# Attention by pairs of heads: both heads' float32 scores and value products alternate between the halves of the array

## The chip, the cores and the metric

One core of one Trainium2 chip. The metric is the device time of one execution in microseconds (us), the median of three runs; lower is better.

## What is computed

Windowed causal attention with a linear bias (4 batches, 8 heads, 576 positions, 64 dimensions per head, window 128), then two dense layers over the 2304 tokens.

```python
scores = q @ k.T / sqrt(64)
scores = where((rel >= 0) & (rel < 128), scores - slope[h] * abs(rel), -1e9)
attn = softmax(scores)                      # per head
x = concat_heads(attn @ v)                  # (2304, 512)
g = x @ w_gate                              # (2304, 1536)
x = (g * sigmoid(g) * (x @ w_val)) @ w_out  # (2304, 512)
h = x @ w_in                                # (2304, 2048)
out = (h * tanh(softplus(h))) @ w_out2      # (2304, 512)
```

## The kernel before, in words

The tokens are cut into five chunks of 512, 384, 512, 512 and 384 (`A_CHUNKS`, line 25), numbered 0 to 4. Per chunk `attention` (L138) makes x, kept as a high and a low float32r half, and the gated layer follows: `gv_groups` (L604) issues 24 hidden groups of 12 matmuls in PSUM tiles `g_ps` (L573), and `out_group` (L637) 12 groups of 12 into `acc`. The attention of chunk 0 runs first and alone ("the start"). After that the attention of chunk c+1 is cut into pieces that are woven between the groups of chunk c's gated layer: the loop at L985 gives out pieces in proportion to their estimated costs. The order on TensorE is written out by hand (`manual_schedule`, L912); a scheduler orders the other engines. Conversions of 64-bit weights to float32 halves (`convert`, L409), on ScalarE and VectorE, are handed out in small steps in between (`pump`). After the gated layer comes a second layer (`layer2`, L756), whose matmuls write tiles `bk`.

`chunk_plan` (L38) cuts a chunk into query blocks of 128 or 64 rows, with 128 to 256 key columns each, packed in PSUM banks of 512 columns. The score columns of a head, by bank, are: chunk 0: 256 and 256, 256 and 128; chunk 1: 256 and 192, 192 and 128; chunk 2: 256 and 256, 256 and 128; chunk 3: 256 and 256, 192, 192 and 128; chunk 4: 256 and 256, 256. Blocks of 192 have 64 query rows. The columns of a head's value products, from key blocks of 128 rows, are: chunk 0: 256, 256, 256, 128; chunk 1: 256, 192, 64; chunk 2: 256, 256, 128, 128, 128; chunk 3: 256, 192, 192, 128; chunk 4: 256, 256, 128, 128. Chunks 1 and 3 have two more blocks of 64 rows and 64 columns each.

The work of a head h has these parts:
- `load` (L147), on the SP queue. In the first `S_FULL` pairs of a chunk (all four in chunk 0, two in chunk 1, none after) a pair of heads is loaded once into 128 partitions, one head in each half of 64. Otherwise each head's q and k are loaded twice, into both halves.
- `split` (L183). For pairs loaded once ScalarE scales q (L188). For the others ScalarE rounds q and k (L196, L124), and VectorE makes what rounding left: the lower half of `Q` (L198) and `KL` (L127).
- `score` (L204), bank by bank into `s_ps`, one of four rotating PSUM banks (`rot`, L119): one float32 product of 64 rows for pairs loaded once; for the others two float32r products over 128 rows, with `K1` and with `KL`. In the trace a float32 product is two MATMULs, a float32r one is one. VectorE adds the bias and takes the minimum (L226), ScalarE makes exponentials with their sums (L230) into `Pt` (10 buffers).
- `norm` (L236): VectorE makes the reciprocals (L238, L241); POOL in chunk 0 (L249) and ScalarE after it (L247) multiply.
- `transp` (L251): TensorE transposes into `t_ps`, ScalarE copies to `PT` (L271).
- `outp` (L274), per pair: the value products, first of one head into partitions 0 to 63 of `o_ps`, then of the other into 64 to 127; ScalarE and VectorE make the halves of x.

`attention_pieces` (L298) orders these as S, T and O pieces by head. In each step "SSOTT" takes the scores of head st, the transposes of the head one before it (two in chunk 0), and the value products one step later again.

Of the kernel before, what the change touches and what calls it, by code (L numbers as in the profile page):

```python
# [9 lines left out]
F32 = mybir.dt.float32  # L10
# [15 lines left out]
S_FULL = [4, 2, 0, 0, 0]  # L26
# [6 lines left out]
    order="SSOTT", delay0=2, early=[4], pbufs=10, pump_g=2, pump_p=2, lag=4, lastlag=6, evprio=500,  # L33
# [4 lines left out]
def chunk_plan(t0, n):  # L38
# [53 lines left out]
    o_order = sorted(kb, key=lambda x: x.par)  # L92
# [4 lines left out]
def body(ctx: ExitStack, tc: tile.TileContext, qT, kT, vP, w1, w1o, w2, cst, yT):  # L97
# [40 lines left out]
    def attention(ap, p, ci, s_native, upfront):  # L138
# [5 lines left out]
        def s_full(h):  # L144
            return h // 2 < s_native

        def load(h):  # L147
            pr, e = divmod(h, 2)
            if s_full(h) and e:
                return  # L150
# [4 lines left out]
            elif s_full(h):  # L155
                q = ap.tile([128, p.n], F32, tag=("qraw", "Q")[pr % 2], name="q32")
                k = ap.tile([128, p.nk], F32, tag=("K1", "KL")[pr % 2], name="k32")
            else:
                q = ap.tile([128, p.n], F32, tag="qraw", name="qraw")
                k = ap.tile([128, p.nk], F32, tag="kraw", name="kraw")  # L160
            for s in p.segs:
                cq, ck = slice(s.c0, s.c0 + s.n), slice(s.koff, s.koff + s.kn0 + s.n)
                sq, sk = slice(s.s0, s.s0 + s.n), slice(s.s0 - s.kn0, s.s0 + s.n)
                if s_full(h):
                    nc.sync.dma_start(out=q[:, cq], in_=qT[s.b, h:h + 2, :, sq].rearrange("h d s -> (h d) s"))
                    nc.sync.dma_start(out=k[:, ck], in_=kT[s.b, h:h + 2, :, sk].rearrange("h d s -> (h d) s"))
                    continue
                for e in range(2):
                    nc.sync.dma_start(out=q[64 * e:64 * e + 64, cq], in_=qT[s.b, h, :, sq])
                    nc.sync.dma_start(out=k[64 * e:64 * e + 64, ck], in_=kT[s.b, h, :, sk])  # L170
            raw[h] = (q, k)
# [11 lines left out]
        def split(h):  # L183
            c = -float(2.0 ** (h - 2))
            if s_full(h):
                if h % 2 == 0:
                    q, k = raw.pop(h)
                    nc.scalar.activation(out=q, in_=q, func=AF.Copy, scale=qsc[:, h // 2:h // 2 + 1])  # L188
                    for e in range(2):
# [888 lines left out]
```

## Time and profile before

| | |
|---|---|
| median of three runs | 1001.56 us (1001.00, 1001.56, 1004.53) |
| span of the profiled execution | 1002.2 us; no other time of it is listed |
| busy: PE, DVE, ACT, POOL | 966.8, 706.7, 555.0, 137.4 us |
| start (chunk 0's attention alone) | 0 to 58.85 us |
| windows with attention woven in | 58.85 to 556.8 us |
| gated layer of chunk 4, then second layer | from 556.8 us |

PE is TensorE's matmuls and PEld its weight loads, DVE VectorE, ACT ScalarE, POOL GpSimd, SP the queue that issues transfers; L117 is a helper through which nearly all matmuls go, so tile names tell them apart. Matmuls overlap: the ends of their records are modelled, so the time that a group takes is read from its first start to the start of what comes next. The granted clock is a share of 2.4 GHz.

### The profile page before, as it was taken

How to read it: one execution, taken by the hardware profiler on the slowest of the kernel's cores; microseconds unless marked ns; L12 is line 12 of the kernel's file. 1: busy time of each engine (PE TensorE's matmuls, PEld its weight loads, DVE VectorE, ACT ScalarE, POOL GpSimd, SP SyncE). 2: the span in 40 equal slices, each digit the busy share in tenths (PEclk: the TensorE clock that was granted, in tenths of full speed). 3: DMA queues.
4: the chain of work that ended last, by engine and by line, in shares of the span. 5: the costliest groups of instructions: out<-in, count | busy, mean ns of one | idle time of the engine just before them, and what ended most of it. 6: DMA issues, size and time to landing. Idle time of an engine off the chain costs nothing. (4 is left out here: it accounts for less than half of the span.)

```text
span 1002.2 us, 14578 instructions
## 1 busy us (share of the span) xinstructions
PE 966.8 (96%) x5168; PEld 854.4 (85%) x5168; DVE 706.7 (71%) x1263; ACT 555.0 (55%) x1135; POOL 137.4 (14%) x204
## 2 busy tenths in 40 slices
PE   6899999999999999999999999899999999999998
PEld 4557777898997877788787999789999999999998
DVE  4989898686586644647843576787795888867773
ACT  6857566666677555544643345555463555545342
POOL 2610000000000000000001233454002330022000
PEclk8989999999999999999999999999999999999999
DMA  8854433566454632326610898432787137850275
GB/s 303 283 208 146 136 120 114 183 214 199 129 166 152 215 110 69 101 65 227 233 43 22 298 374 293 169 116 84 243 260 254 64 109 269 291 172 22 82 248 195
DMA packets 76920, 174.82 MB, mean 174 GB/s; under 512 B 9136, under 2 KB 52528, under 8 KB 67120
## 3 DMA queue, kind: packets, MB, share of 16 engines
q1 hardware_dynamic: 76848, 173.90, 51.9%
q8 instruction: 40, 0.66, 0.3%
q14 instruction: 32, 0.26, 0.1%
HBM read 138.22 MB, written 35.65 MB: 173 GB/s over the span
## 5 line engine op out<-in xcount | busy, mean ns | idle before, releaser
L117 PE MATMUL g_ps<-xt,w 128*128 128x512 f32 (+1 forms) x1440 | 316.4, 372 | 1.1 <-ACT PT L271 1.1
L117 PEld LDWEIGHTS g_ps<-xt,w 128*128 128x128 f32 x1440 | 258.4, 188 | 38.0 <-ACT PT L271 2.2
L117 PE MATMUL bk<-xs,win 128*128 128x384 f32 x1008 | 179.1, 336 | 7.5 <-DVE G L679 5.4
L117 PEld LDWEIGHTS bk<-xs,win 128*128 128x128 f32 x1008 | 174.4, 188 | 11.8 <-DVE G L679 9.0
L117 PE MATMUL bk<-op,wout 128*128 128x384 f32 x1008 | 175.5, 334 | 0.5 <-DMA wout<-w2o 0.5
L117 PEld LDWEIGHTS bk<-op,wout 128*128 128x128 f32 x1008 | 174.8, 188 | 0.8 <-issue 0.8
L117 PE MATMUL acc<-hh,ring 128*128 128x512 f32 (+1 forms) x480 | 149.4, 374 | 1.6 <-DVE ring L127 1.6
L124 ACT ACTIVATE op<-G 128x768 fp32r<-128x768 f32 x84 | 70.8, 846 | 65.6 <-PE bk L117 63.1
L117 PEld LDWEIGHTS acc<-hh,ring 128*128 128x128 f32 x480 | 88.9, 188 | 15.4 <-DVE ring L127 2.3
L127 DVE TENSOR_TENSOR op<-G,op 128x768 fp32r<-128x768 f32 x84 | 80.5, 965 | 26.9 <-ACT op L124 26.3
L117 PE MATMUL acc<-hl,ring 128*128 128x512 f32 (+1 forms) x240 | 88.4, 368 | 0.0
L230 ACT ACTIVATE Pt<-Pt,sm 128x256 f32<-128x256 f32 (+2 forms) x160 | 74.3, 466 | 14.8 <-DVE sm L226 14.5
L613 ACT ACTIVATE t<-g_ps 128x512 f32<-128x512 f32 (+1 forms) x60 | 32.9, 549 | 78.8 <-PE g_ps L117 78.6
L614 DVE SCALAR_TENSOR_TENSOR t<-t,g_ps 128x512 f32<-128x512 f32 (+1 forms) x60 | 37.7, 629 | 53.0 <-ACT t L613 53.0
L226 DVE CUSTOM_DVE_ANT_0 Pt<-s_ps,cst_sb 128x256 f32<-128x256 f32 (+2 forms) x160 | 54.2, 376 | 27.7 <-PE s_ps L117 19.4
L775 POOL TENSOR_TENSOR t<-w 128x256 f32<-128x256 f32 x48 | 42.5, 905 | 224.1 <-DVE win L127 211.3
L622 DVE SCALAR_TENSOR_TENSOR t<-t,g_ps 128x512 f32<-128x512 f32 (+1 forms) x60 | 37.9, 632 | 37.0 <-PE g_ps L117 36.0
L1023 ACT ACTIVATE G<-G 128x384 f32<-128x384 f32 x72 | 36.8, 520 | 44.4 <-DVE G L679 44.4
L679 DVE TENSOR_TENSOR G<-u,bk 128x384 f32<-128x384 f32 x72 | 39.0, 552 | 31.3 <-PE bk L117 29.2
L124 ACT ACTIVATE hh<-t 128x512 fp32r<-128x512 f32 (+1 forms) x60 | 34.9, 582 | 43.8 <-DVE t L622 43.8
L259 PE MATMUL t_ps<-cst_sb,Pt 128*128 128x128 f32 (+2 forms) x288 | 47.0, 279 | 7.7 <-POOL Pt L249 4.2
L247 ACT ACTIVATE Pt<-Pt,sm 128x256 f32<-128x256 f32 (+2 forms) x128 | 50.1, 465 | 7.1 <-DVE sm L241 7.0
(75 smaller groups left out, 1250.8 us busy)
## 6 DMA issues: line engine op xcount, KB each, us to landing
wout<-w2o SPq DMA_DIRECT2D x42, 1024.0 KB, 6.4
wraw<-w SPq DMA_DIRECT2D x16, 1024.0 KB, 5.7
w2o<-chl SPq DMA_DIRECT2D x16, 896.0 KB, 8.7
wst<-w SPq DMA_DIRECT2D x12, 1024.0 KB, 7.4
cw<-w1od SPq DMA_DIRECT2D x24, 512.0 KB, 3.9
w<-w2d SPq DMA_DIRECT2D x24, 512.0 KB, 3.3
w2d<-cw SPq DMA_DIRECT2D x16, 512.0 KB, 4.6
wraw<-w1o SPq DMA_DIRECT2D x6, 1024.0 KB, 6.1
```

Of the source, the lines that this page charges most:

```text
L117: nc.tensor.matmul(out=out, lhsT=lhsT, rhs=rhs, start=start, stop=stop, skip_group_check=True)
L124: return nc.scalar.activation(out=out, in_=in_, func=AF.Copy)
L127: return nc.vector.tensor_tensor(out=out, in0=in_, in1=hi.bitcast(F32), op=ALU.subtract)
L226: nc.vector.tensor_tensor_reduce(out=Pt[:q.qn, :w], in0=s_ps[:q.qn, q.so:q.so + w], in1=nb[:q.qn, 128 - q.kn:128 + q.qn], op0=ALU.add, op1 ...
L230: nc.scalar.activation(out=Pt[:q.qn, :w], in_=Pt[:q.qn, :w], func=AF.Exp, scale=-1.0, bias=sm[:q.qn, i:i + 1], accum_out=sm[:q.qn, 8 + i:9 ...
L247: nc.scalar.activation(out=pt, in_=pt, func=AF.Copy, scale=r)
L259: nc.tensor.transpose(t_ps[:x.n, o:o + q.qn], Pt[:q.qn, c0:c0 + x.n], ident[:q.qn, :q.qn])
L614: nc.vector.scalar_tensor_tensor(out=t[:, :n], in0=t[:, :n], scalar=1.0, in1=st["g"][:, :n], op0=ALU.add, op1=ALU.mult)
L622: nc.vector.scalar_tensor_tensor(out=t[:, :n], in0=t[:, :n], scalar=0.5, in1=vps[:, :n], op0=ALU.mult, op1=ALU.mult)
L679: nc.vector.tensor_tensor(out=out, in0=a, in1=b, op=op)
L775: nc.gpsimd.tensor_tensor(out=x[:, o], in0=a, in1=b, op=ALU.subtract)
L1023: nc.scalar.activation(out=out, in_=in_, func=AF.Mish)
```

## The change

Every pair of heads in every chunk is loaded once and scored in float32, without rounded halves. A score piece takes a bank for both heads of a pair, two PSUM banks, and alternates between the heads block by block. One reciprocal step serves a pair. The value products alternate between the heads too, blocks of 128 rows first. Pieces are ordered by pair: "OSTTSTT" takes the value products of two pairs before, a score bank, transposes of the pair before, and so on. Costs of pieces are worked out anew. `Pt` has 16 buffers, `sm` 3, q and k two each. Cut to its core:

```diff
-    order="SSOTT", delay0=2, early=[4], pbufs=10, pump_g=2, pump_p=2, lag=4, lastlag=6, evprio=500,
+    order="OSTTSTT", early=[2], pbufs=16, pump_g=2, pump_p=2, lag=4, lastlag=6, evprio=500,
...
-    o_order = sorted(kb, key=lambda x: x.par)
+    o_order = sorted(kb, key=lambda x: (x.n != 128, x.par))
...
+                nc.sync.dma_start(out=q[:, cq], in_=qT[s.b, hs_, :, sq].rearrange("h d s -> (h d) s"))
+                nc.sync.dma_start(out=k[:, ck], in_=kT[s.b, hs_, :, sk].rearrange("h d s -> (h d) s"))
+            raw[pr] = (q, k)
...
-            nc.scalar.activation(out=Q, in_=q, func=AF.Copy, scale=c)
-            hi_act(K1, k)
-            nc.vector.scalar_tensor_tensor(
-                out=Q[64:128], in0=q[64:128], scalar=c, in1=Q[64:128].bitcast(F32), op0=ALU.mult, op1=ALU.subtract
-            )
-            lo_dve(KL, k, K1)
-            qk[h] = (Q, K1, KL)
+        def split(pr):
+            q, k = raw.pop(pr)
+            nc.scalar.activation(out=q, in_=q, func=AF.Copy, scale=qsc[:, pr:pr + 1])
+            qk[pr] = (q, k)
+
+        def score(pr, g):
             blocks = p.sb[g][0]
+            s_ps = [rot("s_ps") for _ in range(2)]
...
             for q in blocks:
                 w = q.kn + q.qn
-                    mm(o, Q[:, q.c:q.c + q.qn], K1[:, q.ko:q.ko + w], True, False)
-                    mm(o, Q[:, q.c:q.c + q.qn], KL[:, q.ko:q.ko + w], False, True)
+                for e in range(2):
+                    r = slice(64 * e, 64 * e + 64)
+                    mm(s_ps[e][:q.qn, q.so:q.so + w], Q[r, q.c:q.c + q.qn], K[r, q.ko:q.ko + w], True, True)
...
-            for e in range(2):
-                st = True
-                for x in p.o_order:
-                    c0 = x.uses[0][0].c
+            for i, x in enumerate(p.o_order):
+                c0 = x.uses[0][0].c
+                for e in range(2):
                     mm(
                         o_ps[64 * e:64 * e + 64, c0:c0 + x.w], v[:x.n, x.vi, 64 * e:64 * e + 64],
-                        pt_[2 * pr + e, x.bank][:x.n, x.bo:x.bo + x.w], st, False,
+                        pt_[2 * pr + e, x.bank][:x.n, x.bo:x.bo + x.w], i == 0, False,
                     )
...
+            return (a.ci, sum(max(2 * (q.kn + q.qn), 256) for q in a.p.sb[g][0]) / 1200, f)
...
-            return (a.ci, a.nk * 0.86, f)
+            return (a.ci, a.nk * 0.46, f)
...
-            bufs = {"P": CFG["pbufs"], "sm": 8, "PT0": 2, "PT1": 2}
+            bufs = {"P": CFG["pbufs"], "sm": 3, "PT0": 2, "PT1": 2, "q": 2, "k": 2}
```

## Rows read from the trace of the kernel before

**Rows 1.** The page: its head, and busy time of PE with its share.

```profile
span 1002.2 us, 14578 instructions
...
PE 966.8 (96%) x5168; PEld 854.4 (85%) x5168; DVE 706.7 (71%) x1263; ACT 555.0 (55%) x1135; POOL 137.4 (14%) x204
```

**Rows 2.** Busy time by stage; behind the engines: granted clock, transfers' share, GB/s.

```profile
0.00:58.85 58.85, 43.48 (x184) 29.32 (x184) 42.79 (x118) 41.62 (x102) 27.22 (x52) 0.85 0.88 308
58.85:194.30 135.45, 132.82 (x637) 98.94 (x637) 119.98 (x242) 90.61 (x207) 1.49 (x10) 1.00 0.43 141
194.30:299.70 105.40, 102.73 (x637) 97.68 (x637) 73.74 (x173) 71.20 (x175) 0.83 (x8) 1.00 0.54 169
299.70:436.90 137.20, 137.20 (x674) 106.28 (x673) 75.22 (x173) 75.82 (x196) 0.92 (x6) 1.00 0.38 121
436.90:556.80 119.90, 118.35 (x581) 96.03 (x581) 69.06 (x131) 57.83 (x123) 3.90 (x5) 1.00 0.37 122
```

**Rows 3.** Matmuls of s_ps in two stretches of the start (length, PE busy, count).

```profile
6.58:7.86 1.28, 1.28 (x4) 1.00 0.90 277
7.86:9.14 1.28, 1.28 (x8) 1.00 1.10 287
```

**Rows 4.** The same for o_ps, later in the start.

```profile
34.70:35.38 0.68, 0.68 (x4) 1.00 1.01 364
35.38:36.06 0.68, 0.68 (x8) 1.00 0.99 398
```

**Rows 5.** Matmuls of o_ps by window (length, PE busy, count).

```profile
58.85:194.30 135.45, 13.73 (x81) 1.00 0.43 141
194.30:299.70 105.40, 11.49 (x80) 1.00 0.54 169
299.70:436.90 137.20, 17.07 (x96) 1.00 0.38 121
436.90:556.80 119.90, 8.89 (x64) 1.00 0.37 122
```

**Rows 6.** Timeline of PE (start, length): first and last of five float32 score matmuls.

```profile
30.43 0.38 PE L117 MATMUL s_ps<-qkv 64*128 64x256 f32 x1
...
31.30 0.38 PE L117 MATMUL s_ps<-qkv 64*128 64x256 f32 x1
```

**Rows 7.** Timeline of PE: a rounded head's 512 score columns, to the next group.

```profile
452.74 0.28 PE L117 MATMUL s_ps<-K,Q 128*128 128x256 f32 x1
...
453.22 0.40 PE L117 MATMUL acc<-hh,ring 128*128 128x512 f32 x1
```

**Rows 8.** Timeline of PE: gated groups and float32 scores; an undisturbed run of 24.

```profile
58.86 3.03 PE L117 MATMUL g_ps<-xt,w 128*128 128x512 f32 x12
61.81 1.16 PE L117 MATMUL s_ps<-k,q 64*128 64x256 f32 x4
62.90 0.50 PE L117 MATMUL g_ps<-xt,w 128*128 128x512 f32 x1
...
137.03 5.66 PE L117 MATMUL g_ps<-xt,w 128*128 128x512 f32 x24
142.53 0.27 PE L259 MATMUL t_ps<-cst_sb,Pt 128*128 128x128 f32 x1
```

**Rows 9.** Groups of DVE, 58.85 to 194.30 us (busy, mean ns, idle before).

```profile
L441 DVE SCALAR_TENSOR_TENSOR cw<-cw,cp 128x1024 f32<-128x1024 f32 x15 | 18.2, 1213 | 0.1
...
L127 DVE TENSOR_TENSOR KL<-kraw,K 128x512 fp32r<-128x512 f32 (+1 forms) x7 | 5.2, 741 | 0.1
L198 DVE SCALAR_TENSOR_TENSOR Q<-qraw,Q 64x384 fp32r<-64x384 f32 (+1 forms) x7 | 4.3, 613 | 0.2
```

**Rows 10.** Waits of PE over the span (us in total, times, longest).

```profile
PE s_ps L117 <- DVE Q L198: 2.1, 2, 1.3
```

**Rows 11.** The start: groups of POOL to 58.85 us; timeline of PE, last value products.

```profile
L249 POOL TENSOR_SCALAR Pt<-Pt,sm 128x256 f32<-128x256 f32 (+1 forms) x32 | 25.5, 813 | 25.5 <-ACT qkv L188 10.8 <-DVE sm L241 8.0 <-PE o_ps L117 4.7
...
54.10 4.83 PE L117 MATMUL o_ps<-PT,qkv 128*64 128x256 f32 x16
```

More of the change, by code (lines that the diff above doesn't have):

```diff
@@ L136, in body, with attention, load @@
     x_t = {}
-    def attention(ap, p, ci, s_native, upfront):
+    def attention(ap, p, ci, upfront):
         raw, qk, pt_, P_, sums = {}, {}, {}, {}, {}
         nb_ = len(p.qb)
[L144 to L150, printed above, removed]
+        def load(pr):
             if upfront:
@@ new lines, in norm @@
+        def norm(pr):
+            sm = sums.pop(pr)
+            nc.vector.tensor_scalar(out=sm[:, 16:32], in0=sm[:, 16:32], scalar1=1.0e-9, scalar2=None, op0=ALU.add)
+            nc.vector.reciprocal(out=sm[:, 32:48], in_=sm[:, 16:32])
+            for e in range(2):
+                for q in p.qb:
+                    w = q.kn + q.qn
+                    i = 32 + 8 * e + q.idx
+                    Pt = P_[2 * pr + e, q.idx]
+                    pt, r = Pt[:q.qn, :w], sm[:q.qn, i:i + 1]
+                    if ci:
+                        nc.scalar.activation(out=pt, in_=pt, func=AF.Copy, scale=r)
+                    else:
+                        nc.gpsimd.tensor_scalar(out=pt, in0=pt, scalar1=r, scalar2=1.0, op0=ALU.mult, op1=ALU.mult)
@@ L298, in attention_pieces, with load @@
     def attention_pieces(atts):
-        heads = [(a, h) for a in atts for h in range(H)]
         pairs = [(a, r) for a in atts for r in range(HP)]
-        n = len(heads)
+        n = len(pairs)
         out = []
         def run(k, f):
-            a, h = heads[k]
-            return getattr(a, f)(h)
-        def load(k):
-            if not heads[k][0].upfront:
-                run(k, "load")
-        def load_v(r):
-            if not pairs[r][0].upfront:
-                pairs[r][0].load_v(pairs[r][1])
+            a, r = pairs[k]
+            return getattr(a, f)(r)
+        def load(k, *fs):
+            if not pairs[k][0].upfront:
+                for f in fs:
+                    run(k, f)
         def first():
             if atts[0].upfront:
-                for h in range(0, H, 2):
-                    run(h, "load")
-                    for f in early.pop(h, []):
-                        f()
-            load(0)
-            load_v(0)
+                for r in range(HP):
+                    run(r, "load")
+                    for f in early.pop(r, []):
+                        f()
+            load(0, "load", "load_v")
             run(0, "split")
-            load(1)
-            load_v(1)
+            load(1, "load", "load_v")
         def s_piece(k, g):
-            a, h = heads[k]
+            a, r = pairs[k]
             def f():
@@ L340, in f @@
                         if k + 2 < n:
-                            load(k + 2)
-            return (a.ci, 1.7 if a.s_full(h) else 0.87, f)
+                            load(k + 2, "load")
+            return (a.ci, sum(max(2 * (q.kn + q.qn), 256) for q in a.p.sb[g][0]) / 1200, f)
         def o_piece(k):
-            a, h = heads[k]
+            a, r = pairs[k]
             def f():
```

125 lines of the change are left out of this document (38 added, 87 removed).

## The prediction

> **What bounds the kernel now.** I read the page's busy shares first: TensorE is busy 96% of a span of 1002.2 us [rows 1]. An average hides stages, so next came the table by stage [rows 2]. It has five stages up to 556.8 us: the start, in which the attention of token chunk 0 runs alone, and four windows, in each of which the gated layer of one chunk runs while the attention of the next is woven in. What follows is not touched. The reader is to see three things there. In the start TensorE is busy only 43.48 of 58.85 us, and no engine is full: VectorE 42.79, ScalarE 41.62, at a mean granted clock of 0.85. From 194.3 us on TensorE alone is full (102.73 of 105.40, 137.20 of 137.20, 118.35 of 119.90) and VectorE is at 55 to 70%. In the window from 58.85 to 194.30 us both are close: TensorE 132.82 and VectorE 119.98 of 135.45. So TensorE time taken out of the last three windows is time off the end; in the first it is so only as far as VectorE follows.
>
> **Do halves of the array run side by side?** On this the change stands, and the kernel before already shows it where two neighbouring score groups of heads 0 and 1 meet. Two stretches of equal length hold 4 and then 8 float32 score matmuls [rows 3]: the second head, on the other 64 rows, starts beside the first. The value products show the same for the column halves, where the second head of a pair begins before the first ends: 4, then 8 in 0.68 us [rows 4]. Neither shows a slower pace. It happens only at the seams because all of one head is issued before the other; alternating makes it last through the group.
>
> **Value products (the large gain).** By stage their matmuls are busy 13.73, 11.49, 17.07 and 8.89 us, 51.2 in all [rows 5]. The pace of a float32 matmul of 256 columns comes from two starts four apart, 30.43 and 31.30 [rows 6]: 0.87 / 4 = 0.217 us; each product issues two, so 0.43 us per 256 columns. With both heads abreast a pair costs one head's columns. Chunk 1: 512 columns from 128-row blocks, 0.87 us, and two 64-column blocks of 64 rows, four matmuls at 0.11 (an estimate: twice the column share of 0.217). Chunk 2: 896 columns, 1.52. Chunk 3: 768, 1.30, and again two small blocks. Chunk 4: 768, 1.30. For going in and out I add 0.25 us, and 0.15 for the change from 128 to 64 rows, estimates from the changes of shape below. That is 1.7, 1.8, 2.1 and 1.55 us a pair, times four pairs: 28.6. Gain: 51.2 - 28.6, rounded to **-22 us**. Bounds: -12, if only every other block finds its neighbour, to -25 without the 0.25 and 0.15.
>
> **Scores (a loss on balance).** Chunks 2 to 4 and half of chunk 1 now pay two float32r matmuls per block; a head's 512 columns take 452.74 to 453.22 us, 0.48 [rows 7], or 0.96 for two heads. In float32 the same 512 columns take 4 x 0.217 = 0.87 for both heads together, nearly the same, but changing the array's shape costs. One head's float32 group of 448 columns lasts from 61.81 to 62.90, 1.09 us, of which 0.76 is columns; the 12 matmuls ahead of it last 58.86 to 61.81, 2.95, against half of 5.50 (137.03 to 142.53) where nothing changes shape [rows 8]. So 0.33 + 0.20, with 0.1 for the second head's tail: 0.63 us per group. A pair has two groups. After, per pair: chunk 1: 768 columns, 1.30 + 1.26 = 2.56; chunk 2: 896, 2.78; chunk 3: 1024, 2.99; chunk 4: 768, 2.56; times four, 43.6 us. Before: rounded pairs 1.44, 1.68, 1.92, 1.44; in chunk 1 two pairs were float32 head by head, 2 x (1.30 + 2 x 0.53) = 4.7 each. Sum 9.4 + 2.9 + 4 x 5.04 = 32.5. That is +11; groups whose blocks are all 128 wide spare the second change of shape inside the 0.33, so I take **+8 us**, bounds +3 (changes of shape half hidden) and +11.
>
> **Halves no longer made.** In the first window alone VectorE loses 5.2 + 4.3 = 9.5 us [rows 9]; ScalarE's rounding and the doubled loads of q and k go too. Off the path this is worth nothing by itself, since TensorE covers it. But TensorE waited 2.1 us for those halves [rows 10], and this goes: **-2**. What is late next there is the scale of q, one ScalarE instruction per pair, issued a whole pair ahead.
>
> **VectorE in the first window.** TensorE's work there falls by some 9 us: 7 from value products, 1 from scores, 1 from the wait. VectorE's falls by 9.5 of 119.98, so it stays as full as it was; its conversions, 1.213 us an instruction [rows 9], hold up what TensorE asks for. I give back **+2**, bounds 0 and +8.
>
> **The start.** Its last value product group takes 54.10 to 58.86, 4.76 us, for 16 matmuls, straight before the first gated matmul [rows 8, 11]; abreast, at the same clock, seven units of 0.43 and 0.4 around them, 3.4: -1.4. The other three groups and the scores of four pairs lose about half too, but beside ScalarE and VectorE. Against this, normalising on POOL (32 instructions, 25.5 us, 0.813 each [rows 11]) now follows both heads' scores, so the first transposes can wait for up to four more, 3.3 us, once. Bounds: -10 (TensorE's idle 15.4 us largely closed up) to +6 (late by a head at two stages). I take **-4**, nearer to the last group, whose saving is plain. The remaining edits I cost at nothing. Loads go from two a head and segment, or four, to two a pair; on SP such a load now waits for the scores of two pairs before, to reuse their q and k, and weight loads queue behind it. What hides this is a lead of a whole pair and transfers that fill only 0.37 to 0.54 of the windows [rows 2]; without it a window's conversion would start late, by one load. The sixteen score buffers for ten hold two pairs, as ten held two heads and a half.
>
> The start's clock is a reason for doubt. The row shows a mean of 0.85 of 2.4 GHz before the gated layer and 1.00 in every later window [rows 2]: it stood at 1.2 GHz for part of a stretch with much idle TensorE. The Trainium skill (TensorE: Matmul & The Clock Gate, section Part 1: The HAM clock gate) says that the throttled state is the default and that activity releases it; by that, a start with less matmul work would sit lower still, and the sum would be some 6 us higher. The trace agrees only in that the clock is lower where TensorE idles.
>
> **Sum.** -22 + 8 - 2 + 2 - 4 = -18 on the span of 1002.2, 984.2. The median of the runs shown, 1001.56, lies 0.6 below that span, so **983.5 us**. Everything after 556.8 us moves up unchanged: its weight combinations begin only when the attention's memory is free.
>
> **Rivals.**
> Gains close up further (970 us): start -10, scores +3, nothing given back: -31 in all. For it: every stage of the start waits. Against: VectorE's 120 us in the first window. Chance 0.17.
> Pairs are too coarse (993 us): the start ends 6 later instead of 4 earlier. For it: POOL's chain; against: TensorE and ScalarE have less to do. 0.13.
> The start runs mostly at 1.2 GHz (989.5 us): transposes and value products lie between POOL and the first gated matmul. Price: of the 43.48 us that TensorE is busy some 31 stay; from a clock of 0.85 to 0.5 they take 22 longer, and I count a quarter of that as on the path, as TensorE idles a quarter of the start (15.4 of 58.85) [rows 2]: +6. For it: the clock of 0.85. Against: the scores of both heads, now back to back. 0.07.
> Slower, by PSUM banks (up to 1023 us): a score group of a pair now takes two of the four rotating banks, so the next hidden group or transposes meet a bank sooner that VectorE hasn't read. Place: behind the 32 score groups of the windows. Price: one long conversion, 1.213 us [rows 9], each, 39 us. It decides from 18 / 32 = 0.56 us per group on. For it: the first window, where VectorE is full. Against: the other windows with VectorE at 55 to 70% [rows 2]. 0.05.
> The halves take turns after all (1024 us), and the change doesn't do what it says: value products keep 51.2 us, scores of both heads are paid in full, about +19 more. Against it stand 8 in the place of 4 [rows 3, 4]. 0.03.
>
> **Numbers.** The forecast's case has 0.55, its own range 976 to 991. From the fast rival to the coarse pairs with their bounds the range is 970 to 996; outside lie the last two and some of either end, under 0.2. A measurement of this kernel can tell about 0.5%, 5 us: faster than 996.5 are the forecast, the fast one, the clock and most of the coarse: 0.87; within it 0.07; slower 0.06.
>
> **What would show it.** Value products busy near 29 us over the four windows; a score group of 512 columns for two heads in 1.1 to 1.4 us; no Q or KL rows on VectorE; the gated layer starting near 55 us; the first window near 128 us long, then about 102, 132 and 121. It is wrong if the starts of the two heads' matmuls follow each other instead of pairing, if TensorE's waits for VectorE's reading of score banks grow to over 10 us, or if the start is longer than 58.85.

## The result, and the profile after

The changed kernel takes 1009.2 us in the median of five runs (1007.69 to 1014.23); the kernel before, run again beside it, 1001.56. The ratio is 1.0073, with a 95% interval of 1.0047 to 1.0099: a little slower, where 983.5 us had been forecast. The profiled run is itself the one of 1009.2 us, with a span of 1007.4.

The page of the changed kernel: its head, the busy times, and the granted clock over 40 slices.

```profile
span 1007.4 us, 14079 instructions
...
PE 949.3 (94%) x5168; PEld 828.8 (82%) x5168; DVE 665.8 (66%) x1167; ACT 532.5 (53%) x1093; POOL 133.2 (13%) x184
...
PEclk7889999999999999999999999999999999999999
```

Every engine has less to do than before [rows 1]: TensorE 17.5 us less, VectorE 40.9, ScalarE 22.5. The time grew all the same: over the span TensorE stands idle for 58.1 us, against 35.4 before, so it lies in waits. The table by stage, with the columns PE, PEld, DVE, ACT, POOL, clock, transfers' share and GB/s, says where:

```profile
0.00:62.20 62.20, 35.85 (x185) 22.77 (x185) 42.44 (x110) 42.85 (x103) 25.25 (x43) 0.81 0.79 282
62.20:196.10 133.90, 128.22 (x638) 95.00 (x638) 107.27 (x213) 83.59 (x196) 0.56 (x5) 0.97 0.38 125
196.10:302.80 106.70, 102.58 (x638) 92.94 (x637) 61.47 (x149) 64.70 (x163) 0.45 (x4) 0.98 0.46 150
302.80:435.50 132.70, 131.11 (x674) 99.01 (x673) 67.34 (x153) 69.43 (x185) 0.45 (x4) 1.00 0.34 115
435.50:560.00 124.50, 119.44 (x582) 92.89 (x580) 62.67 (x115) 54.05 (x114) 3.93 (x5) 0.99 0.32 107
```

Against [rows 2] the start is 3.3 us longer (62.20 for 58.85). The four windows together last 497.8 us, against 497.95: nothing was gained. What follows 560 us takes 447.4 us, 2.0 more than before. In the windows TensorE idles 16.4 us (497.8 less the sum of its busy times, 481.4), against 6.9 before; and its clock, which stood at 1.00 in every window, is now 0.97, 0.98, 1.00 and 0.99. Each share missing, times its window, is 4.0 + 2.1 + 0 + 1.2 = 7.4 us of full speed lost, before rounding. I use these two sums, **idle** and **lost clock**, for every kernel below; the shares have two decimals, so a lost clock is good to some 2 us.

The TensorE work itself did become cheaper. The sum over the four windows for the value products:

```profile
sum 497.80, PE 31.27 PEld 19.93 DVE 10.60 ACT 9.24; mean PE 7.82 PEld 4.98 DVE 2.65 ACT 2.31
```

The same for the scores:

```profile
sum 497.80, PE 34.94 PEld 19.76 DVE 41.71; mean PE 8.74 PEld 4.94 DVE 10.43
```

Value products: 31.3 us for the 51.2 of [rows 5]. Scores: 34.9, where the same view of the kernel before sums to 42.5. Counted from the start of a score group to the start of what follows it, with idle time taken off, which leaves overlap out, it is 32.9 against 34.5. What TensorE waits for in the windows (us in total, times, longest):

```profile
PE o_ps L116 <- ACT PT L239: 8.2, 6, 2.9
PE t_ps L227 <- DVE t L569: 4.0, 1, 4.0
PE g_ps L116 <- DVE sm L193: 1.4, 2, 0.7
PE t_ps L227 <- ACT Pt L215: 1.2, 1, 1.2
PE s_ps L116 <- DVE t L577: 1.0, 1, 1.0
```

And the largest in the start:

```profile
PE t_ps L227 <- POOL Pt L217: 17.2, 9, 6.0
```

The largest in the windows is new: the value products wait for `PT`, the copies of the transposes. Three of the others, 4.0, 1.4 and 1.0 us, are waits for a PSUM bank that VectorE has not read yet. A wait for `PT` on TensorE's timeline (start, length; in brackets the wait and what ended it):

```profile
320.95 0.91 PE L227 MATMUL t_ps<-cst_sb,Pt 128*128 128x128 f32 x4
...
324.75 0.97 PE L116 MATMUL o_ps<-PT,v 128*64 128x256 f32 x6
326.81 1.46 PE L116 MATMUL o_ps<-PT,v 128*64 128x192 f32 x18 [1.09 <-ACT PT L239]
```

ScalarE's timeline beside it:

```profile
322.78 3.66 ACT L215 ACTIVATE Pt<-Pt,sm 128x256 f32<-128x256 f32 x10
326.34 0.53 ACT L239 ACTIVATE PT<-t_ps 128x320 f32<-128x320 f32 x2
```

The transposes are done by 321.86, but ScalarE copies them only at 326.34. Ahead of the copies in its queue stand the ten normalisations of the next pair, 3.66 us in one burst. Some of these waits TensorE pays for a second time. The table of TensorE around a wait of 2.90 us for the same copies (length, busy, clock, transfers):

```profile
286.00:289.90 3.90, 3.90 (x26) 1.00 0.26 92
289.90:294.10 4.20, 1.30 (x13) 0.97 0.00 0
294.10:297.50 3.40, 3.40 (x17) 0.54 0.14 36
297.50:301.00 3.50, 3.50 (x22) 1.00 0.27 76
```

After 2.90 idle of 4.20 us the granted clock is 0.54 for the next 3.40 us, near the lower of its two levels, 1.2 GHz, with TensorE busy all the time; then it is full again.

### The profile page after: what moved, and what is told of

Its sections match the earlier page's. It is cut to its first block, busy times and chain, and to the rows that moved or that the text cites. A ratio compares the mean times of both kernels' runs of the same rounds, so it can differ in the third digit from the quotient of the medians.

```text
span 1007.4 us, 14079 instructions
## 1 busy us (share of the span) xinstructions
PE 949.3 (94%) x5168; PEld 828.8 (82%) x5168; DVE 665.8 (66%) x1167; ACT 532.5 (53%) x1093; POOL 133.2 (13%) x184
## 4 chain that ended last, share of the span: by engine, by line
PE 72%; DVE 8%; DMA 8%; ACT 6%; issue 3%; POOL 2%; SPq 1%; DVEq 0%; ACTq 0%; POOLq 0%
PE bk L116 30%; PE g_ps L116 24%; PE acc L116 11%; DMA wraw<-w 4%; PE o_ps L116 2%; PE s_ps L116 2%; PE t_ps L227 2%; ACT Pt L215 2%; ACT Pt L198 1%; POOL Pt L217 1%; POOL t L730 1%; DVE cw L390 1%; DMA x2d<-ev 1%; DMA w<-w2d 1%; DVE G L634 1%
## 5 line engine op out<-in xcount | busy, mean ns | idle before, releaser
L116 PE MATMUL g_ps<-xt,w 128*128 128x512 f32 (+1 forms) x1440 | 320.3, 376 | 1.4 <-DVE sm L193 1.4
L116 PE MATMUL acc<-hh,ring 128*128 128x512 f32 (+1 forms) x480 | 153.2, 382 | 1.6 <-DVE ring L126 1.6
L116 PEld LDWEIGHTS acc<-hh,ring 128*128 128x128 f32 x480 | 90.5, 191 | 16.4 <-DVE ring L126 2.3
L198 ACT ACTIVATE Pt<-Pt,sm 128x256 f32<-128x256 f32 (+2 forms) x160 | 74.2, 465 | 30.8 <-DVE sm L193 30.7
L227 PE MATMUL t_ps<-cst_sb,Pt 128*128 128x128 f32 (+2 forms) x288 | 51.2, 290 | 22.7 <-POOL Pt L217 17.2
L126 DVE TENSOR_TENSOR hl<-t,hh 128x512 fp32r<-128x512 f32 (+1 forms) x60 | 40.1, 669 | 47.3 <-ACT hh L123 47.3
L568 ACT ACTIVATE t<-g_ps 128x512 f32<-128x512 f32 (+1 forms) x60 | 32.9, 548 | 71.3 <-PE g_ps L116 71.2
L227 PEld LDWEIGHTS t_ps<-cst_sb,Pt 128*128 128x128 f32 (+2 forms) x288 | 34.8, 144 | 42.5 <-POOL Pt L217 22.4
L577 DVE SCALAR_TENSOR_TENSOR t<-t,g_ps 128x512 f32<-128x512 f32 (+1 forms) x60 | 37.7, 628 | 36.5 <-PE g_ps L116 35.4
```

What stands on the lines that cost most here:

```text
L116: nc.tensor.matmul(out=out, lhsT=lhsT, rhs=rhs, start=start, stop=stop, skip_group_check=True)
L126: return nc.vector.tensor_tensor(out=out, in0=in_, in1=hi.bitcast(F32), op=ALU.subtract)
L198: nc.scalar.activation(out=Pt[:q.qn, :w], in_=Pt[:q.qn, :w], func=AF.Exp, scale=-1.0, bias=sm[:q.qn, i:i + 1], accum_out=sm[:q.qn, 16 + i: ...
L227: nc.tensor.transpose(t_ps[:x.n, o:o + q.qn], Pt[:q.qn, c0:c0 + x.n], ident[:q.qn, :q.qn])
L568: tanhs.append(nc.scalar.activation(out=t[:, :n], in_=st["g"][:, :n], func=AF.Tanh, scale=0.5))
L577: nc.vector.scalar_tensor_tensor(out=t[:, :n], in0=t[:, :n], scalar=0.5, in1=vps[:, :n], op0=ALU.mult, op1=ALU.mult)
```

## The experiments

Times are medians; every ratio is against the kernel before, run on the same chip. Windows means the sum of the four windows.

### Which part pays, and which costs

**e3: the kernel before, with the value products alternating and nothing else.**

```diff
-    o_order = sorted(kb, key=lambda x: x.par)
+    o_order = sorted(kb, key=lambda x: (x.n != 128, x.par))
...
-            for e in range(2):
-                st = True
-                for x in p.o_order:
+            for i, x in enumerate(p.o_order):
+                for e in range(2):
...
-            return (a.ci, a.nk * 0.86, f)
+            return (a.ci, a.nk * 0.46, f)
```

> The kernel before with one part of the change: value products alternate between the heads, blocks of 128 rows first, piece cost 0.46; scores, order by head and buffers as before. Theory (the gain of 22 us of TensorE time is real and is kept where value products stand a head's step behind their transposes): value products busy near 30 us in the windows, under 9 us idle on TensorE there, time 983 (979 to 988). Rival (VectorE and transfers set the pace of the windows): time 996 to 1001.

981.84 us, ratio 0.9821 [0.9773, 0.9869]. The sum of its windows by engine:

```profile
sum 474.80, PE 469.39 PEld 384.93 DVE 335.87 ACT 292.33 POOL 7.12; mean PE 117.35 PEld 96.23 DVE 83.97 ACT 73.08 POOL 1.78
```

The same for its value products alone:

```profile
sum 474.80, PE 26.64 PEld 17.38 DVE 10.62 ACT 9.09; mean PE 6.66 PEld 4.34 DVE 2.65 ACT 2.27
```

The windows are 23.2 us shorter than before, for 24.5 us of value products: here the gain reaches the end. Idle 5.4, lost clock 2.0.

**e4: the changed kernel, with the value products head by head again** (the same lines, reversed).

> The changed kernel with the value products one head after the other again, as before the change. Theory (their halved time was mostly given back as waits for PT copies, which a longer first head would cover): waits of value products fall under 2 us and no stretches at 1.2 GHz follow them; TensorE works 20 us longer; time 1016 (1012 to 1021). Rival (the gain is kept in full and the 27 us that are missing are lost elsewhere): 1027 to 1032.

1035.89 us, ratio 1.0333 [1.0308, 1.0358]; both figures missed, and the rival's by less. The value products are worth 26.7 us in the pairs' order too. So it is the rest, the pairs' scores and their order, that costs some 30.

**e9: e3 with float32 scores in all chunks, head after head.**

```diff
-S_FULL = [4, 2, 0, 0, 0]
+S_FULL = [4, 4, 4, 4, 4]
```

> The best version so far (value products alternating, scores and order by head as before, 981.8 us) with float32 scores in all five chunks, head after head: the rounded halves of q and k are gone here too, but the steps stay those of one head. The run with the pairs' scores head after head (1019.5 us) has the same score matmuls in the order by pairs. Theory (the order by pairs is what costs, not the float32 scores): the four windows stay near 475 us; blocks of 64 rows double the pace of their groups, which added 10.5 us to the windows of that run, half of it here since chunk 1 had half of its heads so already; 2 to 3 us of waits for the halves go: 985 us, between 980 and 992. Rival (the float32 scores, or what VectorE and ScalarE do in the freed time, cost it): 1000 to 1015 us, with the stretches at 1.2 GHz in the windows and waits for VectorE as in the changed kernel.

1019.11 us, ratio 1.0169 [1.0139, 1.02]: above both. Of the rival's two reasons it is the first, the scores themselves; the waits for VectorE that it named don't come. Idle stays at 5.3 us, but the scores take TensorE 66.75 us, against 42.85 in e3. The sum over its windows for the scores:

```profile
sum 511.00, PE 66.75 PEld 37.58 DVE 43.77; mean PE 16.69 PEld 9.39 DVE 10.94
```

The windows grow by 36.2 us against e3. From start to start the scores take 61.6 us of them, for 33.7 in e3, and the groups between them the other 8.

**e5: the changed kernel, with the score matmuls of one head after those of the other** inside a step.

```diff
-            for q in blocks:
-                w = q.kn + q.qn
-                for e in range(2):
+            for e in range(2):
+                for q in blocks:
+                    w = q.kn + q.qn
```

> The changed kernel with the score matmuls of a piece in turn: first all blocks of one head, then all of the other, in the same two banks. Theory (TensorE looks some four matmuls ahead, so in a short group the second head starts while the first head's last matmuls still wait, with or without alternation): a group of 512 columns for two heads stays under 1.4 us for 1.06, time 1008 to 1014. Rival (only alternation makes the halves run side by side): such a group takes 1.9 us, 32 groups some 25 us, time 1030 to 1036.

1019.45 us, ratio 1.0172 [1.0141, 1.0203], between the two. Groups of blocks of 128 rows don't mind (1.07 us for 1.06); those with blocks of 64 rows double (2.41 for 1.22). So the alternation is needed for float32 scores to cost TensorE no more than rounded ones, and it delivers that. The loss must come from somewhere else.

### Repairs of the changed kernel

**e1: value products behind the first two transposes, three buffers for `PT`** (the start as it was).

```diff
+    order="STTOSTT", order0="OSTTSTT", early=[2], pbufs=15, pump_g=2, pump_p=2, lag=4, lastlag=6, evprio=500,
...
+            for c in CFG["order0"] if st < 5 else CFG["order"]:
...
+            bufs = {"P": CFG["pbufs"], "sm": 3, "PT0": 3, "PT1": 3, "q": 2, "k": 2}
```

> The changed kernel, but outside the start the value products of a pair come after a score bank and two transposes of the next pair (STTOSTT), with three PT buffers a bank for two and 15 score buffers for 16. Theory (in the windows the saved TensorE time went into waits of value products for the PT copies on ScalarE, 8.2 us, and into the stretches at 1.2 GHz that such gaps bring): these waits fall under 2 us, two of the four stretches at 1.2 GHz in the windows go, time 997 (994 to 1001). Rival (VectorE and the transfers of weights set the pace of the windows, and TensorE would wait elsewhere): the waits turn up at transposes and score banks, time 1007 to 1011.

999.25 us, ratio 0.9973 [0.9956, 0.999], the time as expected. Windows 490.7. The waits for `PT` go, and TensorE waits 5.1 us for VectorE's reading of score banks and 2.9 for normalisations in their place. The clock gains nothing: the shares of the windows are 0.96, 1.00, 0.99 and 1.00, a lost clock of 6.8 us.

**e2: both score steps of a pair ahead of the transposes, in the start only** (`order0="OSSTTTT"`).

> The changed kernel, but in the start both score banks of a pair come before the transposes of the pair before it (OSSTTTT for chunk 0). Theory (in the start the second score bank stands behind transposes that wait for POOL, so each pair's scores, exponentials, normalising and transposes follow each other in one chain): the start ends at 56 to 59 us for 62.2, time 1004 (1002 to 1007). Rival (the start is bound by the amount of work on ScalarE, VectorE and POOL): it ends at 61 to 63, time 1008 to 1010.

1005.16 us (995.21 to 1008.96), ratio 1.0028 [0.9999, 1.0057], the median as expected. The start of its profiled run ends at 58.6 instead of 62.2: GpSimd's bursts begin 4 to 6 us earlier from the second pair on, and TensorE waits 8.0 us for them instead of 17.2. But this run is the slowest of the ten; its windows last 501.6 us, and at their end, 560.2 us, nothing of the gain is left.

**e6: normalising on GpSimd in all chunks** (`if False:` for `if ci:` ahead of the normalisation).

> The changed kernel with the normalising of the weights on POOL in all chunks, for ScalarE outside the start. Theory (a pair's eight to ten normalising instructions, 3.7 us in one block, stand on ScalarE ahead of the PT copies that the value products wait for): waits of value products fall from 8.2 us in the windows to under 2.5, time 1000 (996 to 1004). Rival (those copies are late because of conversions and exponentials on ScalarE, or POOL slows VectorE as much): waits stay over 5 us or come up elsewhere, time 1006 to 1013.

1010.24 us, ratio 1.0078 [1.0057, 1.0098]. The waits for `PT` fall to nearly nothing, as the theory said, and the time doesn't move: 6.5 us for VectorE's gate and 5.1 for its score banks take their place.

**e7: e1, e2 and e6 together.**

> The changed kernel with three edits of order together: value products later in the windows, both score banks first in the start, normalising on POOL. Theory (what the change lost, some 28 us against alternating value products alone, is all waits of the order by pairs and the clock that follows them; float32 scores by halves cost no more than rounded ones): 988 (983 to 993). Rival (float32 scores themselves cost over 8 us in the windows, by changes of shape and a lower clock): 994 to 1002.

1003.47 us, ratio 1.0028 [1.0002, 1.0054]. The theory falls, and the rival is just missed. The repairs don't add up, and e1 alone is faster: the start ends at 57.3, but the first window grows to 138.9.

**e10: the normalisations spread, four behind each step**, of the 6 to 10 that a pair has (the text below says 16, wrongly).

```diff
-                        nc.scalar.activation(out=pt, in_=pt, func=AF.Copy, scale=r)
+                        todo_n.append((2 * pr + e, pt, r))
...
+            def f():
+                a.transp(2 * r + e, g)
+                some(k + e, 4)
```

> The changed kernel with the 16 normalisations of a pair, after the first chunk, no longer issued in one burst behind the last score step, but four behind each of the steps that follow; the work is the same, on the same engine. Theory (bursts: ScalarE is held 4 to 6 us by one step of a pair, so the gate's work hh and the copies PT come late, VectorE waits 42 us for hh in the windows against about 9 with heads, and TensorE then waits): VectorE's waits for hh fall to about half, TensorE's idle time in the windows from 16 us to 8, its stretches at 1.2 GHz from four to two at most: 997 us, between 990 and 1002. Rival (any order by pairs moves the wait to the next buffer, as the two earlier repairs showed): the waits for PT go and others come, 1003 to 1011 us.

1001.84 us, ratio 1.0007 [0.9984, 1.003]. Inside the theory's range, but not by its road: VectorE's waits for `hh`, the gate's rounded result that ScalarE makes, stay at 41.8 us, TensorE's waits for `PT` at 6.5, and idle at 14.0.

**e11: the same on top of e1.**

> The same spreading on top of the version with the value products moved behind the first transposes and three buffers for transposed P (999.3 us). Theory (bursts): both repairs add up: 990 us, between 984 and 996. Rival (the wait moves on): 996 to 1003 us.

997.64 us, ratio 0.9965 [0.9944, 0.9987]; windows 488.3. The rival holds.

**e8: e3, with every other block of chunk 0 normalised on ScalarE.**

> Alternating value products alone in the kernel before, with half of the start's normalising (odd query blocks) on ScalarE for POOL. Theory (the start's transposes wait 8 us for POOL): the start ends at 55 to 58 us for 60.0, time 979 (976 to 982). Rival (ScalarE is as late, the same chain): 982 to 985.

984.2 us, ratio 0.9829 [0.9784, 0.9875]: no gain over e3, as the rival said.

### What it is in the pairs' scores

**e12: e3, in the order by pairs behind the first chunk**, with 16 buffers for the scores; every instruction as it was.

```diff
+    order="SSOTT", order2="OSSTTSSTT", delay0=2, early=[4], pbufs=16, pump_g=2, pump_p=2, lag=4, lastlag=6, evprio=500,
...
+                    elif h % 2:
+                        a.norm(h - 1)
+                        a.norm(h)
```

> The best version so far (value products alternating, scores of one head at a time with rounded halves, 981.8 us), with the steps behind the first chunk set out by pairs as in the changed kernel: both heads' scores, then the 16 normalisations of both in one burst, the transposes of both one pair-step later and the value products two later, 16 buffers for the scores; every instruction is the same as before, only the order differs, and each score step still takes one bank. Theory (the grain of pairs costs, not the pairs' float32 scores): TensorE's idle time in the four windows goes from 5 us to 10 or more, waits for the copies PT or the gate's halves come up, and the windows go from 475 us to 488 to 500: 1000 us, between 994 and 1008. Rival (the order alone costs little; what costs is the pair's score step, which takes two banks at once and holds VectorE and ScalarE with eight blocks): the windows stay within 6 us of 475: 984 us, between 980 and 990.

983.54 us, ratio 0.9828 [0.9808, 0.9849]; windows 477.4. The rival holds. But the burst that the expectation speaks of didn't come about: the scheduler of ScalarE's queue put the first head's normalisations ahead of the second head's exponentials, since nothing holds them there. So this run is no test of such a burst.

**e13: e12, with the two score steps of a head made one** (`order2="OSTTSTT"`): a head's three to five blocks (not eight, as the text below has it) and two banks at once.

> The version with heads' scores, rounded halves and the order by pairs (983.5 us), with the two score steps of a head made one step behind the first chunk: eight blocks and two banks are taken at once, and VectorE and ScalarE get eight reductions and eight exponentials in a row, as in the pair's step of the changed kernel; the instructions are the same, and the score matmuls are still the rounded ones. Theory (the double score step is what costs): waits for VectorE or ScalarE come up at the steps behind it, TensorE's idle time in the windows goes from 7 us to 12 or more, stretches at 1.2 GHz appear there, and the windows go from 477 to 488 to 500 us: 998 us, between 992 and 1006. Rival (the step's size costs nothing; something in the float32 pair scores themselves does): windows within 5 us of 477: 984 us, between 979 and 989.

978.82 us, ratio 0.9773 [0.9744, 0.9802]: the rival by its windows, the time a touch below its range. This is the **lowest median** of the study, though the intervals of e3, e8 and e16 overlap with its own. Its windows:

```profile
52.40:177.10 124.70, 124.70 (x638) 96.26 (x638) 117.76 (x241) 89.33 (x207) 1.43 (x10) 1.00 0.45 152
177.10:279.30 102.20, 100.33 (x638) 95.68 (x637) 73.41 (x174) 71.34 (x175) 0.83 (x8) 0.98 0.59 188
279.30:407.90 128.60, 128.54 (x673) 102.09 (x672) 78.56 (x177) 76.06 (x197) 0.63 (x6) 1.00 0.43 136
407.90:527.00 119.10, 117.03 (x581) 93.77 (x580) 67.57 (x130) 57.33 (x123) 2.85 (x4) 1.00 0.38 123
```

Windows 474.6, idle 4.0, lost clock 2.0. The start ends at 52.4 us, for 60.0 in e3, which has the same order in it but 10 score buffers for 16.

**e14: the changed kernel, with each score step cut in two along its blocks** (`order="OSSTTSSTT"`, the second half in the banks of the first).

> The changed kernel with each score step cut in two along its blocks: the first half takes the two banks, and the matmuls, reductions and exponentials of half of the blocks of both heads come in it, the others one step later; a step then holds as much as one of the heads' steps. Theory (the double score step is what costs): the windows go from 498 to 480 to 488 us, and the start may move by 3 us either way: 994 us, between 986 and 1000. Rival (two banks held together cost it, however the work in them is cut, or the float32 pair scores do): 1002 to 1012 us, and the stretches at 1.2 GHz in the windows stay.

1035.77 us, ratio 1.0327 [1.0288, 1.0367]; outside both, and not a test of the question. The cut brings a wait of its own: the matmuls of the second half wait until VectorE has read the first from the same banks, `s_ps` behind `sm`, 18.5 us in 21 waits.

**e15: the changed kernel, with twice the planned cost of a score step**, and **e16: e13 with half of it.**

```diff
-            return (a.ci, sum(max(2 * (q.kn + q.qn), 256) for q in a.p.sb[g][0]) / 1200, f)
+            return (a.ci, sum(max(2 * (q.kn + q.qn), 256) for q in a.p.sb[g][0]) / 600, f)
```

> The changed kernel with one number changed: the cost at which a score step is entered in the plan that spreads the steps over a window is doubled (the divisor 1200 becomes 600), so that more of the layer's own groups run behind a score step, before the transposes and the value products that need what VectorE and ScalarE make of it. In the best version so far (978.8 us) the plan has 3.5 us of score steps to a pair's 7.2, in the changed kernel 1.7 of 5.5. Theory (the plan's cover behind the score step is what costs): waits for PT fall under 3 us, stretches at 1.2 GHz in the windows to one or two, the windows go from 498 to 478 to 486 us: 992 us, between 986 and 998. Rival (something else in the float32 pair scores): 1002 to 1011 us, windows above 490.

> The best version so far (heads' scores in steps of two banks, the order by pairs, 978.8 us) with the plan's cost of a score step halved, to the level of the changed kernel. Theory (the plan's cover behind the score step): waits for PT and for VectorE come up, TensorE's idle time in the windows goes from 4 us to 10 or more: 988 us, between 983 and 1000. Rival (the plan's cost doesn't matter): 976 to 982 us.

1008.06 us, ratio 1.005 [1.0033, 1.0066], and 980.23, ratio 0.9777 [0.975, 0.9804]. Both rivals hold: doubling and halving the planned cost move the median by 1.1 and 1.4 us.

**e17: e13, with one tile of sums and one reciprocal for both heads of a pair.**

```diff
+            if g == 0 and (ci == 0 or h % 2 == 0):
+                sums[h] = ap.tile([128, 48], F32, tag="sm", name="sm")
...
+                if ci:
+                    sums[h + 1] = sums[h]
...
+            if ci == 0 or h % 2 == 0:
...
+                nc.vector.reciprocal(out=sm[:, 32:48], in_=sm[:, 16:32])
```

> The best version so far (heads' scores in steps of two banks, the order by pairs, 978.8 us), with one tile of sums and one reciprocal for both heads of a pair behind the first chunk, as in the changed kernel. In the trace of that version the normalisations of the first head run between the two score steps; now none can start before the last exponential of the pair, and all of them come in one burst on ScalarE. Theory (the sums that are shared by the pair cost: the burst stands ahead of the copies PT, for which the value products wait): waits for PT of 5 us or more, stretches at 1.2 GHz in the windows, windows from 475 to 487 to 500: 998 us, between 989 and 1006. Rival (the burst costs little, the float32 pair matmuls cost it): windows within 5 us of 475: 979 us, between 976 and 985.

994.51 us (987.14 to 998.48), ratio 0.9913 [0.9876, 0.9949]. The theory holds. Its windows:

```profile
61.20:185.80 124.60, 124.60 (x638) 96.44 (x637) 113.36 (x224) 86.76 (x203) 0.45 (x4) 1.00 0.42 135
185.80:293.50 107.70, 101.50 (x638) 95.58 (x637) 74.20 (x168) 74.12 (x180) 0.56 (x4) 0.98 0.55 176
293.50:428.70 135.20, 131.90 (x673) 104.32 (x673) 77.87 (x169) 75.86 (x197) 0.00 (x0) 0.97 0.41 130
428.70:550.40 121.70, 118.25 (x581) 94.65 (x580) 67.65 (x124) 57.32 (x123) 2.86 (x4) 0.99 0.37 120
```

Its largest wait of TensorE in them:

```profile
PE o_ps L117 <- ACT PT L276: 10.5, 7, 2.9
```

ScalarE's timeline in the pair that begins its third window, the normalisations and copies:

```profile
309.12 2.68 ACT L252 ACTIVATE Pt<-Pt,sm 128x256 f32<-128x256 f32 x7
...
312.65 1.08 ACT L252 ACTIVATE Pt<-Pt,sm 64x192 f32<-64x192 f32 x3
313.63 0.63 ACT L276 ACTIVATE PT<-t_ps 128x448 f32<-128x448 f32 x2
...
315.75 0.51 ACT L276 ACTIVATE PT<-t_ps 128x320 f32<-128x320 f32 x2
```

ScalarE's timeline of the same pair in e13:

```profile
288.06 1.89 ACT L247 ACTIVATE Pt<-Pt,sm 128x256 f32<-128x256 f32 x5
...
290.21 0.54 ACT L271 ACTIVATE PT<-t_ps 128x320 f32<-128x320 f32 x2
...
294.81 1.88 ACT L247 ACTIVATE Pt<-Pt,sm 128x256 f32<-128x256 f32 x5
...
297.54 0.63 ACT L271 ACTIVATE PT<-t_ps 128x448 f32<-128x448 f32 x2
300.72 0.54 ACT L271 ACTIVATE PT<-t_ps 128x320 f32<-128x320 f32 x2 [2.55 <-PE t_ps L259]
```

With separate sums five normalisations run between the score steps and five behind them; with shared sums all ten come at the end, right ahead of the copies. The windows grow by 14.6 us (489.2 for 474.6), of which idle is 9.0 (13.0 for 4.0) and lost clock 5.4 (7.4 for 2.0). TensorE waits 10.5 us for `PT` instead of 1.2. These sizes come from one execution of each kernel, here the slowest of five, in e13 the fastest of four. This run of e17 has a start of 61.2 us for 52.4 as well, which this edit doesn't explain; the medians differ by 15.7.

**e18: the changed kernel, with a tile of sums, a reciprocal and the normalisations for each score step.**

```diff
-            if g == 0:
-                sums[pr] = ap.tile([128, 48], F32, tag="sm", name="sm")
+            sm = sums[pr, g] = ap.tile([128, 48], F32, tag="sm", name="sm")
...
                 a.score(r, g)
+                a.norm(r, g)
```

> The changed kernel with a tile of sums, a reciprocal and the normalisations for each score step, in place of one for both steps of a pair: the blocks of the first step no longer wait for the exponentials of the second. Two small instructions more on VectorE for each pair. Theory (the sums shared by the pair's two steps cost): waits for PT under 3 us, at most two stretches at 1.2 GHz in the windows, windows from 498 to 476 to 486, and the start 2 to 4 us shorter, since GpSimd's chain begins a step earlier: 988 us, between 980 and 996. Rival (the float32 pair matmuls cost it): 1001 to 1010 us.

1000.34 us, ratio 0.998 [0.997, 0.9991], between the two. The sum of its windows, and its wait for `PT` in them:

```profile
sum 490.00, PE 478.16; mean PE 119.54
...
PE o_ps L116 <- ACT PT L237: 1.2, 2, 1.1
```

The waits for `PT` fall from 8.2 us to 1.2, as the theory said; the windows go to 490.0, not to 476 to 486, and the start doesn't shorten (63.8). Idle is 11.8, now spread over seven kinds of wait, none above 2.6 us in all, and the lost clock stays (shares of 0.99, 0.98, 1.00 and 0.97).

## Why the prediction was wrong

The forecast had the span at 984.2 us; it is 1007.4. Of the 23.2 us the start missed 7.3 (62.2 for 54.9), the windows 13.9 (497.8 for 483.9), and the part behind them 2.0.

**Value products, -22: right.** Their busy time fell by 19.9 us in the changed kernel and by 24.5 in e3, and both e3 against the kernel before and the changed kernel against e4 show it in the time. Halves of the array do run side by side, and the rival in which they take turns is out.

**Scores, +8: wrong, on the safe side.** From start to start the scores take 1.6 us less, not 8 more. The failing term is the 0.63 us per group for changes of shape: a pair's 512 columns were to take 0.87 + 0.63 = 1.50 us and take 1.06. The term came from one head's group with blocks of 64 rows, 1.09 us [rows 8]; a pair's group of the same blocks takes 1.10, so the second head costs next to nothing. So by the sum the windows should have come out shorter than forecast, at 474 us, which only versions with rounded scores reach (e3, e13).

**"TensorE time taken out of the last three windows is time off the end", and "the remaining edits I cost at nothing": these two failed together.** One remaining edit was that one reciprocal serves a pair. The forecast weighed it for GpSimd in the start, and gave it no term in the windows. In e17 it alone costs 14.6 us of windows. The chain: the sums of both score steps and both heads share a tile, so no block is normalised before the last exponential of the pair; ScalarE gets all normalisations in one burst, behind which the copies `PT` queue; the value products wait; and the clock falls after some of the waits. In the changed kernel, a tile for each score step, still shared by the two heads (e18), gives back 7.8 us of windows and 8.9 of the median.

**What stays open.** Against e13 the changed kernel's windows are 23.2 us longer: idle 12.4, lost clock 5.4, and 5.4 in the groups themselves. Shared sums explain 8 to 15 of it, by e18 and e17, if the size in e17 holds here too. The rest shows as small waits, of which two places can be named; the 2.0 us behind the windows were not traced. The first window lasts 129.0 us in e18 and 124.7 in e13. In the last one the transposes wait 4.00 us for a bank that VectorE has not read. TensorE's timeline of the changed kernel:

```profile
487.41 0.65 PE L227 MATMUL t_ps<-cst_sb,Pt 128*128 128x128 f32 x4 [4.00 <-DVE t L569]
```

VectorE's, up to that point:

```profile
486.06 0.69 DVE L385 TENSOR_SCALAR cw<-wraw 128x1024 int32<-128x1024 int32 x1 [2.91 <-DMA wraw<-w]
486.67 0.68 DVE L569 SCALAR_TENSOR_TENSOR t<-t,g_ps 128x512 f32<-128x512 f32 x1
```

At the head of VectorE's queue stands a weight conversion whose transfer is late, and the gate's multiplication behind it. This goes when the value products come later (e1 and e11, whose last window lasts 117 us). The loads of whole pairs, which the forecast also cost at nothing, were not tested alone. In the windows they hold up SP's queue for 93.2 us, waiting for scores; in e9, which loads pairs too, it is 109.3 us, and the windows idle only 5.3. No version with the pairs' float32 scores came below 997.6 us (e11), and none was run in which each head and step has its own sums, so a cost of the pairs' step itself is not excluded. Why the pairs' order meets such waits more often wasn't settled; that each repair brought up the next wait (e1, e6, e7) fits many small leads used up at once, but that is argued, not shown.

**VectorE in the first window, +2: not the bound.** VectorE is busy 117.76 of 124.70 us there in e13, with TensorE never idle. It follows.

**The start, -4: +3.3.** By the forecast's own sign, a start longer than 58.85 us, it was wrong. The rival of the coarse pairs had it 6 later, for the right reason: TensorE waits 17.2 us for GpSimd's normalising. Eight of these on GpSimd's timeline:

```profile
29.77 6.67 POOL L217 TENSOR_SCALAR Pt<-Pt,sm 128x128 f32<-128x128 f32 x8 [8.52 <-DVE sm L207]
```

The transposes that want them, on TensorE's:

```profile
32.02 0.48 PE L227 MATMUL t_ps<-cst_sb,Pt 128*128 128x128 f32 x1 [5.99 <-POOL Pt L217]
```

GpSimd itself waits 8.52 us for the pair's reciprocal. The order is part of it: a pair's second score step stands behind transposes that wait for GpSimd, and with both steps first (e2) the start ended at 58.6. Shared sums are another part, and a small one: e18 brought TensorE's waits for GpSimd from 17.2 us to 13.6, and the start no earlier to its end. I had taken the value between the bounds by the last group of value products, whose saving (4.76 us before, 58.93 to 62.16, 3.23, now) did come, and not by the chain that the other bound rested on. The clock moved too: 0.81 for 0.85, or 11.8 us of full speed lost instead of 8.8. The Trainium skill (TensorE: Matmul & The Clock Gate, section Part 1: The HAM clock gate) has the slow state as the one that activity must release. The trace agrees in direction only: TensorE is busy 35.85 us of the start instead of 43.48, and the clock fell by 0.04, not to the 0.5 from which the forecast worked out its 6 us. Both shares are too high, since the first 10 us count at 1.00 [rows 3] though the score matmuls there start 0.43 us apart (7.02 and 7.45 in the kernel before), twice the 0.217 of [rows 6], as at the lower level. The forecast weighed the clock for the start only. In the windows, where I had no term for it, 7.4 us of full speed went.

**PSUM banks, the rival on the slow side: small, not out.** TensorE's waits for a bank that VectorE has not read come to 6.4 us in the windows (the transposes' 4.0, 1.4 and 1.0), against 3.1 before, where the rival had up to 39; and e13 takes two banks at once at no cost. The side was right; the larger part that the runs show goes back to another shared resource, the tile of sums.

## What to carry to other kernels

Work of two heads that fits the two halves of the array should alternate: 20 to 25 us of value products went, and float32 scores became as cheap as rounded ones. But when two units are merged into one, look at what they now share: a common tile of sums turns two small bursts into one, and an engine that works in order then makes unrelated copies wait. Of the versions run, e13 has the lowest median: heads' scores as before, alternating value products, the order by pairs, 978.8 us. It is not clear of e3, which has the alternating value products alone, 981.8.

## What was not expected of the hardware

A float32 score group on one half of the array costs as much as on both: four matmuls of one head, two blocks of 256 columns, take 1.01 to 1.06 us in e9, eight of two heads 1.06 to 1.07, whether they alternate or not. With blocks of 64 rows, in which the matmuls of a head change shape, the order decides: 1.22 us alternating, 2.41 head after head, where the second head starts behind the first.

A wait of 2.90 us was followed by 3.40 us at a mean clock of 0.54, in the middle of a window, behind a stretch in which TensorE was busy all the time. Nor does it take so long a wait. The same table of the changed kernel around one of 1.18 us:

```profile
78.00:82.20 4.20, 2.95 (x16) 1.00 0.78 279
82.20:85.60 3.40, 3.40 (x10) 0.50 0.71 272
```

The kernel before has a wait of 1.3 us [rows 10], and e12 one of 1.7, and the clock stands at 1.00 in all their windows. In e3 it stands at 1.00 in a window with a wait of 2.3 us:

```profile
PE s_ps L117 <- DVE Q L198: 2.3, 1, 2.3
...
60.00:188.60 128.60, 126.23 (x639) 95.38 (x637) 116.05 (x237) 87.94 (x206) 1.73 (x9) 1.00 0.39 127
```

So the length of a wait alone doesn't tell what it costs.
